# Second tile begun behind the first, a third unit ahead of the first tile, and weight steps placed behind the last bias

## The chip, the cores and the metric

One core of one Trainium2 chip runs the kernel. The metric is device microseconds of one launch. The engines are named as in the profile: PE is TensorE (matmul), PEld its weight load, DVE is VectorE, ACT is ScalarE, POOL is GpSimd, SP is the queue that issues most DMAs.

## What is computed

```python
# attention with random features, 4 batches, 8 heads, 576 rows, head size 64
def phi(x):
    proj = np.einsum('bhsd,md->bhsm', x, omega)
    sq = np.sum(x * x, axis=-1, keepdims=True) / 2.0
    h = proj - sq
    h = h - np.max(h, axis=-1, keepdims=True)
    return np.exp(h) / np.sqrt(m)
q_p, k_p = (phi(q_s), phi(k_s))
kv = np.einsum('bhsm,bhsd->bhmd', k_p, v)
z = np.sum(k_p, axis=2)
num = np.einsum('bhsm,bhmd->bhsd', q_p, kv)
den = np.einsum('bhsm,bhm->bhs', q_p, z)[..., None] + 1e-06
x = (num / den)                       # as 2304 rows of 512
# first network: 512 -> 2048 -> 512
h = x @ w_in
g = h * (1.0 / (1.0 + np.exp(-1.702 * h)))
x = g @ w_out
# second network: 512 -> 1536 -> 512
out = (x @ w_a) * (x @ w_b) @ w_out2
```

## The kernel before

Every product is made with numbers split in two halves of 16 bits, high and low: three matmuls (high by high, high by low, low by high) add up in one PSUM bank.

The rows of attention's result are cut in tiles: tile j (0 to 3) holds the first 512 rows of batch j, tile 4 the 256 rows that are left of all batches. The first network takes a tile in 16 units (`ffn1`, line 613). `h_products` (617) makes a unit's 12 matmuls, three for each of four chunks of xT, into a bank of the ring (two banks); chunk c of xT comes from part c (`hp`) of the Q phase. `h_unit` (627) adds the activation: tanh on ACT, `th` on DVE, `gh` on ACT, `gl` (the remainder) on DVE. `y_unit` (647) adds the unit to the tile's four sums y, 12 matmuls in the four banks of `ps_acc`. `main` (658) is a generator: y_unit(f), yield, h_unit(f + 2), yield. So two units are ahead. At the last two units there is no h_unit(f + 2); `main` then calls `after()`, which builds the next tile, and takes the next tile's first two units there. For the step from tile 0 to tile 1 (`j == 1`) these are split: chunks 0 to 2 of unit 0 behind y_unit(14), and its last chunk and unit 1 behind y_unit(15).

Attention of batch b + 1 runs beside tile b. `run` (1023) walks the tile's generator; after each yield it takes weight steps (`w_steps`) and one `side_step`, which moves each live phase of attention on by one yield. There are four K phases (`kphase32`) and four Q phases (`qphase`) in a batch, started two yields apart. Each begins with `features` (366): the input is split, transposed, squared and projected; `mx` is the row maximum (DVE, 470), `mh` and `nb` give the bias of the exponentials (DVE, 476), and ACT makes the exponentials (437). The projections go into one of the two banks of `ps_att` and the exponentials free it. The Q phase ends with the normalised result, whose transpose by DMA (603) writes xT. Batch 0's phases have run before tile 0; batch 1 is computed with the Q side in 32 bits, and its transposes of the exponentials are on PE.

Weights come as 34 chunks of 1 MB: 16 for `w_in` and `w_out` in turn (`NW1`), 4 for the first third of `w_a` and `w_b` (up to `NWE` = 20), 2 of the second network's output weights and 4 more of `w_a`, `w_b` (up to `NW2` = 26), and 8 later. The generator `w_ops` (203) converts them: `shift` (DVE, 214) and two passes that put the number's bits together (DVE, 254 and 262, on 128x1024), for the second network `sums` (DVE, 248), the high half on ACT (272), and the low half (DVE, 221). It yields four or five times for a chunk. `w_load` (196) issues the load on SP (line 200) into one of two buffers, two chunks ahead. `w_steps(n, upto)` takes n steps, `w_need(n)` all that are left up to chunk n. Tile 0 runs with one step at a yield, and so do tile 1 (to chunk 18, 12 steps) and tile 2 (to chunk 20, 10 steps), so that theirs are taken in the first yields, and tile 3 (to 26, 31 steps).

The framework that issues the program orders each engine's instructions itself, from the program's order and the dependencies. `tc.issue_after(ins)` adds that those instructions of the block that run on the engine of `ins` (here DVE) are queued behind `ins`; it adds no semaphore. In `run` it is used for tiles 1 and 2, with the last instruction of the batch before (`own["last", b - 1]`).

The second network (`ffn2`, 763) runs behind tile 4. A product's bank is copied by ACT into `ka`, `kb` (`keep`, 789), totals are added on DVE, and `ab_forms` (823) makes from two groups' results seven slots of high (ACT, 836) and low halves (DVE, 837), by `split` in pieces of two, two, two and one slot.

Of the kernel before, what the change touches and what calls it, by code (L numbers as in the profile page):

```python
# [9 lines left out]
F32 = mybir.dt.float32  # L10
# [23 lines left out]
def fused_kernel(  # L34
# [13 lines left out]
    nc = tc.nc  # L48
# [4 lines left out]
    P = 128  # L53
    NT = 4
    SM = NT * P
    SR = S - SM
    NHP = H // 2
    KC = DM // P
    FC1 = F1 // P
# [15 lines left out]
    first = ExitStack()  # L75
# [32 lines left out]
    RW = CW // P  # L108
# [58 lines left out]
    NW1 = len(chunks)  # L167
# [117 lines left out]
    def w_steps(n, upto):  # L285
        for _ in range(n):
            if w_done[0] < upto:
                w_done[0] = next(w_gen)

    def w_need(n):  # L290
        while w_done[0] < n:
            w_done[0] = next(w_gen)
# [73 lines left out]
    def features(pool, nm, x, e16, e32, psp, extra):  # L366
# [88 lines left out]
        for gi in range(len(GROUPS) + 2):  # L455
            if e32 is None:
                for gj in [x for x in es if x not in done]:
                    parts(gj)
                    done.append(gj)
            if 1 <= gi <= len(GROUPS):  # L460
                g, pv = GROUPS[gi - 1], pvs[gi - 1]
                pair = PAIRS[gi - 1]
                a, z = GROUPS[pair[0]][0], GROUPS[pair[-1]][-1] + 1
                if pair[0] not in mxs:
                    mxs[pair[0]] = [
                        pool.tile([P, T], F32, tag=t, name=f"{t}_{nm}_{gi}", bufs=2)
                        for t in ("mx", "mh", "nb")
                    ]
                mx, mh, nb = mxs[pair[0]]
                nc.vector.tensor_reduce(  # L470
                    out=mx[:, g[0] - a : g[-1] + 1 - a], in_=pv[:, : len(g), :], axis=AX.X, op=ALU.max
                )
                if gi - 1 == pair[-1]:

                    for o, i0, scale in ((mh, mx, PROJ), (nb, mh, -1.0)):
                        nc.vector.scalar_tensor_tensor(
                            out=o[:, : z - a], in0=i0[:, : z - a], scalar=scale, in1=sq[:, a:z],
                            op0=ALU.mult, op1=ALU.subtract,
                        )
                    for gj in pair:  # L480
                        exps(gj, nb, a)
            if gi < len(GROUPS):
                pvs[gi] = pv = psp().rearrange("p (t m) -> p t m", m=M)
                project(pv, GROUPS[gi])
            yield
# [127 lines left out]
    def ffn1(j, xh, xl, n):  # L613

        gh, gl, yacc, phs = {}, {}, {}, {}

        def h_products(f, cs):
            if f not in phs:
                phs[f] = ps_ring.tile([P, 512], F32, tag="ring", name=f"ph{j}_{f}")
            ph = phs[f]  # L620
            w, fs = w_in[f // 8], slice(f % 8 * P, (f % 8 + 1) * P)
            for c in cs:
                nc.tensor.matmul(ph[:, :n], w[:, 0, c, fs], xh(c), start=(c == 0), stop=False)  # L623
                nc.tensor.matmul(ph[:, :n], w[:, 0, c, fs], xl(c), start=False, stop=False)  # L624
                nc.tensor.matmul(ph[:, :n], w[:, 1, c, fs], xh(c), start=False, stop=(c == KC - 1))  # L625

        def h_unit(f, cs=range(KC)):
            h_products(f, cs)
            ph = phs.pop(f)
            th = mp.tile([P, 512], F32, tag="f32", name=f"th{j}_{f}")  # L630
            nc.scalar.activation(  # L631
                out=th[:, :n], in_=ph[:, :n], func=AF.Tanh, scale=0.5 * 1.702 / (S_X * S_W)
            )
            nc.vector.scalar_tensor_tensor(  # L634
                out=th[:, :n], in0=th[:, :n], scalar=1.0, in1=ph[:, :n], op0=ALU.add, op1=ALU.mult
            )
            GS = 0.5 * S_G / (S_X * S_W)
            a = gp.tile([P, 512], F16, tag="gh", name=f"gh{j}_{f}")
            b = gp.tile([P, 512], F16, tag="gl", name=f"gl{j}_{f}")
            nc.scalar.activation(out=a[:, :n], in_=th[:, :n], func=AF.Copy, scale=GS)  # L640
            nc.vector.scalar_tensor_tensor(  # L641
                out=b[:, :n], in0=th[:, :n], scalar=GS, in1=a[:, :n],
                op0=ALU.mult, op1=ALU.subtract,
            )
            gh[f], gl[f] = a, b

        def y_unit(f):
            w = w_out[f // 4]
            for c in range(KC):
                if f == 0:  # L650
                    yacc[c] = ps_acc.tile([P, 512], F32, tag="acc", name=f"y{j}_{c}")
                cs = slice(c * P, (c + 1) * P)
                o = yacc[c][:, :n]
                nc.tensor.matmul(o, w[:, 0, f % 4, cs], gh[f][:, :n], start=(f == 0), stop=False)  # L654
                nc.tensor.matmul(o, w[:, 0, f % 4, cs], gl[f][:, :n], start=False, stop=False)  # L655
                nc.tensor.matmul(o, w[:, 1, f % 4, cs], gh[f][:, :n], start=False, stop=(f == FC1 - 1))  # L656

        def main(after=None):

            following = None  # L660
            for f in range(FC1):
                w_need(2 * (f // RW) + 2)
                y_unit(f)
                if f + 1 == FC1:
                    yd = ydram.tile([P, KC, 512], F32, tag=f"y{j}", name=f"yd{j}")
                    for c in range(KC):
                        ye = mp.tile([P, 512], F32, tag="f32", name=f"ye{j}_{c}")
                        nc.scalar.activation(out=ye[:, :n], in_=yacc[c][:, :n], func=AF.Copy, scale=YS)
                        nc.sync.dma_start(out=yd[:, c, :n], in_=ye[:, :n])
                    ys[j] = yd  # L670
                yield
                if f + 2 < FC1:
                    w_need(2 * ((f + 2) // RW) + 1)
                    h_unit(f + 2)
                    yield
                elif after is not None:
                    if following is None:
                        following = after()
                    _, last_rows, products, unit = following
                    if not last_rows:  # L680
                        unit(f + 2 - FC1)
                    elif f + 2 == FC1:
                        products(0, range(KC - 1))
                    else:
                        unit(0, (KC - 1,))
                        unit(1)
                    yield

        return main, j == 1, h_products, h_unit

# [70 lines left out]
    def ffn2():  # L763
# [59 lines left out]
        def ab_forms(k):  # L823
# [9 lines left out]
                nc.vector.tensor_tensor(out=o[:, :n], in0=x[:, :n], in1=y[:, :n], op=op)  # L833

            def split(slots, x):
                nc.scalar.copy(t[:, 0, slots], x)  # L836
                nc.vector.tensor_tensor(out=t[:, 1, slots], in0=x, in1=t[:, 0, slots], op=ALU.subtract)

            put(cb[:, 0], ca[:, 1], ca[:, 2], ALU.add)
# [180 lines left out]
    def begin(t, gen):  # L1020
        waiting.append((turn[0] + t, gen))

    def run(gen, wn=0, wmax=0, after=None):
        for _ in gen:
            if after is None:
                w_steps(wn, wmax)
            else:
                with tc.issue_after(after):
                    w_steps(wn, wmax)
            side_step()  # L1030

    def finish_side():
# [29 lines left out]
    def xparts(xT):  # L1062
        return lambda c: xT[:, c, 0, :], lambda c: xT[:, c, 1, :]
# [27 lines left out]

    following = []

    def next_tile(make):
        def made():
            finish_side()
            following.append(make())
            return following[-1]

        return made  # L1100

    xT = x_tile(0, zp, "z")
    with tc.tile_pool(name="att", bufs=2) as att:
# [18 lines left out]
        fillers(FILL)  # L1122
        w_steps(POST_W, NW1)
        following.append(ffn1(0, *xparts(xT), SM))
        _, _, products, unit = following[0]
        w_need(1)
        for f in range(2):
            products(f, range(KC - 1))
        for f in range(2):
            unit(f, (KC - 1,))  # L1130
        for b in range(1, B):
            x1 = x_tile(b, zp, "z")
            begin_k(b, att, psp_att, 0, AL, b == 1)
            begin_q(b, att, x1, psp_att, NHP * AL, AL, b == 1)
            last = own["last", b - 1]
            run(
                following[-1][0](next_tile(lambda: ffn1(b, *xparts(x1), SM))),
                1, (NW1, NW1 + 2, NWE)[b - 1], last.ins if b > 1 else None,
            )
    late["pool"] = ctx.enter_context(tc.tile_pool(name="late", bufs=1))  # L1140
    run(following[-1][0](next_tile(rest_tile)), 1, NW2)
    w_need(NW2)
    y_load(0, SM)
    fg = y_forms(0, SM)
    for _ in following[-1][0]():
        next(fg, None)
    for _ in fg:
        pass
    first.close()
    late["sums"] = ctx.enter_context(tc.tile_pool(name="sums", bufs=1, side="right", reuse_waits="tile"))  # L1150
    ffn2()
# [36 lines left out]
```

## Time and profile before

| | |
|---|---|
| median of 3 runs | 920.68 us (918.95 to 921.78) |
| profiled execution | 919.44 us |
| its span | 917.7 us |
| granted PE clock, mean | 0.998 |
| busy: PE, DVE, ACT | 885.5, 679.0, 442.0 us |

The profiled execution's time is the span and 1.74 us around it. Busy times of PE overlap from one matmul to the next; idle times don't. A wait is written as "engine tile line <- who released it: us in total, times, longest". Attention of batch 0 fills the first 58 us; tile 0 goes to about 190 us, tile 1 to 298, tile 2 to 406, tile 4 ends at 532, and the second network takes the rest.

### The profile page before, as it was taken

Reading aid. Unit: us, or ns where it says so; the run is one execution under the profiler, and the core shown is the slowest. Engines: PE = TensorE matmul, PEld = TensorE weight load, DVE = VectorE, ACT = ScalarE, POOL = GpSimd, SP = SyncE. Lnnn points to the kernel's source line nnn. Section 1 sums busy time; section 2 is a strip of 40 time slices with the busy share of each in tenths; the row PEclk is TensorE's granted clock in tenths of the full one; section 3 lists DMA queues with packets and bytes.
Section 4 is the critical chain, followed back from the end, with each engine's and each line's share of the span. In section 5 each row is a group of like instructions: output and inputs, shape, how many; then the busy total and the mean of one; then the engine's idle time right before and its main releaser. Section 6 shows DMA issues by size and latency. Waiting matters only on the chain.

```text
span 917.7 us, 17145 instructions
## 1 busy us (share of the span) xinstructions
PE 885.5 (96%) x6984; PEld 639.0 (70%) x6984; DVE 679.0 (74%) x1220; ACT 442.0 (48%) x1047; POOL 1.7 (0%) x11
## 2 busy tenths in 40 slices
PE   8989999989999999999999999999999999999997
PEld 6864555635654466544447888888988888988886
DVE  5889998488678966779932389876999567566756
ACT  6675787556664566554423355543543232233221
POOL 0000000000000000000000000000000000000000
PEclk9999999999999999999999999999999999999999
DMA  7855578263576524554421043223330122223312
GB/s 180 230 146 170 169 224 265 74 104 72 133 151 136 177 56 72 95 141 136 182 82 46 1 162 119 103 90 121 128 126 11 72 41 82 81 93 127 75 47 70
DMA packets 129344, 105.35 MB, mean 115 GB/s; under 512 B 97777, under 2 KB 111089, under 8 KB 127217
## 3 DMA queue, kind: packets, MB, share of 16 engines
q1 hardware_dynamic: 128960, 103.96, 40.2%
q8 instruction: 55, 0.90, 0.4%
q10 hardware_dynamic: 304, 0.30, 0.1%
q14 instruction: 25, 0.20, 0.1%
HBM read 71.07 MB, written 17.69 MB: 97 GB/s over the span
## 4 chain that ended last, share of the span: by engine, by line
PE 54%; DVE 28%; ACT 7%; DMA 6%; issue 4%; SPq 0%; ACTq 0%; DVEq 0%
PE y L654 3%; PE y L655 3%; PE ph L623 3%; PE ph L624 3%; PE y L656 3%; PE ph L625 3%; PE pa L503 2%; DVE wf L254 2%; DVE wf L262 2%; DMA xt_k<-x_k 2%; DVE ca L810 2%; DVE sx L248 2%; PE oA L880 2%; PE oA L878 2%; DVE th L634 2%
## 5 line engine op out<-in xcount | busy, mean ns | idle before, releaser
L655 PE MATMUL y<-gl,w_out 128*128 128x512 f16 (+1 forms) x320 | 114.3, 358 | 2.0 <-DVE gl L641 2.0
L656 PE MATMUL y<-gh,w_out 128*128 128x512 f16 (+1 forms) x320 | 114.3, 358 | 0.0
L654 PE MATMUL y<-gh,w_out 128*128 128x512 f16 (+1 forms) x320 | 111.7, 358 | 0.1
L623 PE MATMUL ph<-xT,w_in 128*128 128x512 f16 x256 | 97.5, 381 | 3.0 <-DMA xT<-x_q_2x 1.4
L624 PE MATMUL ph<-xT,w_in 128*128 128x512 f16 x256 | 97.5, 381 | 0.3 <-DVE xT L592 0.3
L625 PE MATMUL ph<-xT,w_in 128*128 128x512 f16 x256 | 97.5, 381 | 0.0
L634 DVE SCALAR_TENSOR_TENSOR th<-th,ph 128x512 f32<-128x512 f32 (+1 forms) x80 | 50.2, 629 | 53.9 <-ACT th L631 53.9
L631 ACT ACTIVATE th<-ph 128x512 f32<-128x512 f32 (+1 forms) x80 | 44.5, 557 | 68.1 <-PE ph L625 67.9
L640 ACT ACTIVATE gh<-th 128x512 f16<-128x512 f32 (+1 forms) x80 | 46.8, 586 | 48.4 <-DVE th L634 48.1
L785 PE MATMUL paA<-forms,w_a 128*128 128x256 f16 (+1 forms) x240 | 60.9, 262 | 2.6 <-ACT ka L793 2.3
L886 DVE SCALAR_TENSOR_TENSOR o<-oA,o 128x512 f32<-128x512 f32 (+1 forms) x45 | 28.5, 634 | 46.3 <-PE oA L880 46.2
L785 PE MATMUL pbA<-forms,w_b 128*128 128x256 f16 (+1 forms) x240 | 61.1, 262 | 1.1 <-DVE cb L804 1.0
L641 DVE SCALAR_TENSOR_TENSOR gl<-th,gh 128x512 f16<-128x512 f32 (+1 forms) x80 | 50.5, 633 | 15.0 <-ACT gh L640 14.9
L787 PE MATMUL pbA<-forms,w_b 128*128 128x256 f16 (+1 forms) x240 | 61.0, 262 | 0.0
L786 PE MATMUL pbA<-forms,w_b 128*128 128x256 f16 (+1 forms) x240 | 61.0, 262 | 0.0
L787 PE MATMUL paA<-forms,w_a 128*128 128x256 f16 (+1 forms) x240 | 61.0, 262 | 0.0
L786 PE MATMUL paA<-forms,w_a 128*128 128x256 f16 (+1 forms) x240 | 61.0, 262 | 0.0
L878 PE MATMUL oA<-w_o,ab 128*128 128x256 f16 x216 | 58.9, 273 | 1.7 <-ACT ab L836 0.9
L880 PE MATMUL oA<-w_o,ab 128*128 128x256 f16 x216 | 58.9, 273 | 0.2
L879 PE MATMUL oA<-w_o,ab 128*128 128x256 f16 x216 | 58.9, 273 | 0.0
L624 PEld LDWEIGHTS <-w_in 128*128 128x128 f16 x320 | 31.6, 99 | 31.1 <-issue 4.5
L656 PEld LDWEIGHTS <-w_out 128*128 128x128 f16 x320 | 31.3, 98 | 31.0 <-issue 3.9
(195 smaller groups left out, 2302.4 us busy)
## 6 DMA issues: line engine op xcount, KB each, us to landing
wraw<-in_moe_w_out_dram SPq DMA_DIRECT2D x14, 1024.0 KB
forms<-fd SPq DMA_DIRECT2D x8, 1792.0 KB
wraw<-in_moe_w_in_dram SPq DMA_DIRECT2D x8, 1024.0 KB
fd<-forms SPq DMA_DIRECT2D x4, 1792.0 KB
wraw<-in_moe_w_a_dram SPq DMA_DIRECT2D x6, 1024.0 KB
wraw<-in_moe_w_b_dram SPq DMA_DIRECT2D x6, 1024.0 KB
rawk<-in_k_dram SPq DMA_DIRECT2D x16, 256.0 KB
vt<-in_v_dram SPq DMA_DIRECT2D x16, 256.0 KB
```

The source lines that it names most:

```text
L623: nc.tensor.matmul(ph[:, :n], w[:, 0, c, fs], xh(c), start=(c == 0), stop=False)
L624: nc.tensor.matmul(ph[:, :n], w[:, 0, c, fs], xl(c), start=False, stop=False)
L625: nc.tensor.matmul(ph[:, :n], w[:, 1, c, fs], xh(c), start=False, stop=(c == KC - 1))
L634: nc.vector.scalar_tensor_tensor(out=th[:, :n], in0=th[:, :n], scalar=1.0, in1=ph[:, :n], op0=ALU.add, op1=ALU.mult)
L654: nc.tensor.matmul(o, w[:, 0, f % 4, cs], gh[f][:, :n], start=(f == 0), stop=False)
L655: nc.tensor.matmul(o, w[:, 0, f % 4, cs], gl[f][:, :n], start=False, stop=False)
L656: nc.tensor.matmul(o, w[:, 1, f % 4, cs], gh[f][:, :n], start=False, stop=(f == FC1 - 1))
L785: nc.tensor.matmul(o[:, i], wh, xh, start=first, stop=False, skip_group_check=True)
L786: nc.tensor.matmul(o[:, i], wh, xl, start=False, stop=False, skip_group_check=True)
L787: nc.tensor.matmul(o[:, i], wl, xh, start=False, stop=final, skip_group_check=True)
L878: nc.tensor.matmul(bank[:, t], lh, wh, start=first, stop=False, skip_group_check=True)
L880: nc.tensor.matmul(bank[:, t], ll, wh, start=False, stop=final, skip_group_check=True)
```

## The change

1. The `nb` instruction is kept in `own["nb"]`, and `run` queues the DVE instructions of every weight step behind the last `nb` made so far, for all tiles (before: tiles 1 and 2 alone, behind the last instruction of the batch before).
2. `run` takes a rate in place of a count: 1 step a yield in tile 0, 11/32 in tiles 1 and 2, 22/32 in tile 3; tile 4 takes a step at every second yield, and `w_need(NW2)` moves from before tile 4 to behind it.
3. `head` makes a tile's first units: the products of all of them without the last chunk, then the last chunks. Tile 0 gets three units in it; the third has a bank of `ps_acc`, and `w_need` for its weights goes before it. `main(first=3)` then leaves h_unit(2) out.
4. Tile 0 runs to its end without `after`; tile 1 is built and its two units made behind it, with `head`.
5. `split` in `ab_forms` copies each slot by an ACT instruction of its own.

```diff
@@ features
-                        nc.vector.scalar_tensor_tensor(
+                        own["nb"] = nc.vector.scalar_tensor_tensor(
                             out=o[:, : z - a], in0=i0[:, : z - a], scalar=scale, in1=sq[:, a:z],
                             op0=ALU.mult, op1=ALU.subtract,
-                        )
+                        ).ins
@@ ffn1
-        def h_products(f, cs):
+        def h_products(f, cs, pool=ps_ring, tag="ring"):
             if f not in phs:
-                phs[f] = ps_ring.tile([P, 512], F32, tag="ring", name=f"ph{j}_{f}")
+                phs[f] = pool.tile([P, 512], F32, tag=tag, name=f"ph{j}_{f}")
...
-        def main(after=None):
+        def main(after=None, first=2):
...
-                if f + 2 < FC1:
+                if first <= f + 2 < FC1:
                     w_need(2 * ((f + 2) // RW) + 1)
                     h_unit(f + 2)
                     yield
-                elif after is not None:
+                elif f + 2 >= FC1 and after is not None:
                     if following is None:
                         following = after()
-                    _, last_rows, products, unit = following
-                    if not last_rows:
-                        unit(f + 2 - FC1)
-                    elif f + 2 == FC1:
-                        products(0, range(KC - 1))
-                    else:
-                        unit(0, (KC - 1,))
-                        unit(1)
+                    following[2](f + 2 - FC1)
                     yield
@@ ab_forms
             def split(slots, x):
-                nc.scalar.copy(t[:, 0, slots], x)
+                for i in range(slots.stop - slots.start):
+                    nc.scalar.copy(t[:, 0, slots.start + i], x[:, i])
@@ run
-    def run(gen, wn=0, wmax=0, after=None):
+    def run(gen, rate, wmax):
+        due = 0.0
         for _ in gen:
-            if after is None:
-                w_steps(wn, wmax)
-            else:
-                with tc.issue_after(after):
-                    w_steps(wn, wmax)
+            due += rate
+            with tc.issue_after(own["nb"]):
+                w_steps(int(due), wmax)
+            due -= int(due)
             side_step()
@@ new
+    def head(tile, units):
+        _, products, unit = tile
+        for f in range(units):
+            w_need(2 * (f // RW) + 1)
+            if f < 2:
+                products(f, range(KC - 1))
+            else:
+                products(f, range(KC - 1), ps_acc, "acc")
+        for f in range(units):
+            unit(f, (KC - 1,))
@@ the tiles
-        _, _, products, unit = following[0]
-        w_need(1)
-        for f in range(2):
-            products(f, range(KC - 1))
-        for f in range(2):
-            unit(f, (KC - 1,))
+        head(following[0], 3)
         for b in range(1, B):
...
-            last = own["last", b - 1]
-            run(
-                following[-1][0](next_tile(lambda: ffn1(b, *xparts(x1), SM))),
-                1, (NW1, NW1 + 2, NWE)[b - 1], last.ins if b > 1 else None,
-            )
+            ahead = next_tile(lambda: ffn1(b, *xparts(x1), SM))
+            if b == 1:
+                run(following[-1][0](first=3), 1, NW1)
+                ahead()
+                head(following[-1], 2)
+            else:
+                run(following[-1][0](ahead), 11 / 32, (NW1 + 2, NWE)[b - 2])
     late["pool"] = ctx.enter_context(tc.tile_pool(name="late", bufs=1))
-    run(following[-1][0](next_tile(rest_tile)), 1, NW2)
-    w_need(NW2)
+    run(following[-1][0](next_tile(rest_tile)), 22 / 32, NW2)
     y_load(0, SM)
     fg = y_forms(0, SM)
-    for _ in following[-1][0]():
+    for i, _ in enumerate(following[-1][0]()):
         next(fg, None)
+        if i % 2:
+            w_steps(1, NW2)
     for _ in fg:
         pass
+    w_need(NW2)
```

## Rows read from the trace of the kernel before

**Rows 1.** The page's first part: TensorE's busy us, share, instructions.

```profile
PE 885.5 (96%) x6984; PEld 639.0 (70%) x6984; DVE 679.0 (74%) x1220; ACT 442.0 (48%) x1047; POOL 1.7 (0%) x11
```

**Rows 2.** Busy us by stretch: stretch, length, each engine, granted clock, DMA share, GB/s.

```profile
92.00:119.00 27.00, 24.81 (x162) 14.41 (x162) 24.62 (x40) 20.65 (x83) 0.00 (x0) 1.00 0.61 182
119.00:170.00 51.00, 50.59 (x332) 29.21 (x330) 42.89 (x79) 34.84 (x126) 0.00 (x0) 1.00 0.71 204
...
192.00:222.00 30.00, 27.36 (x151) 13.17 (x151) 25.90 (x50) 17.23 (x37) 0.00 (x0) 1.00 0.48 98
222.00:290.00 68.00, 66.71 (x527) 38.95 (x526) 46.26 (x119) 40.37 (x108) 0.00 (x0) 1.00 0.59 117
...
400.00:460.00 60.00, 58.58 (x270) 26.20 (x268) 58.93 (x91) 29.95 (x51) 0.00 (x0) 1.00 0.53 174
460.00:531.00 71.00, 70.93 (x517) 50.32 (x515) 21.15 (x43) 21.61 (x47) 0.00 (x0) 1.00 0.10 35
```

**Rows 3.** TensorE's waits, 58 to 70 us: total, times, longest.

```profile
PE pa L590 <- DVE xf_q L562: 1.1, 1, 1.1
PE ph L623 <- DVE th L634: 0.6, 1, 0.6
```

**Rows 4.** TensorE's waits, 60 to 190 us, on the exponentials.

```profile
PE pa L406 <- ACT e_k L437: 2.3, 3, 0.9
```

**Rows 5.** TensorE's waits, 170 to 192 us, on DMAs.

```profile
PE ph L623 <- DMA xT<-x_q_2x: 1.4, 1, 1.4
PE ph L623 <- DMA xT<-x_q_3x: 0.9, 1, 0.9
...
PE pa L406 <- DMA xt_k<-x_k: 0.5, 1, 0.5
```

**Rows 6.** TensorE's longest waits, 190 to 480 us.

```profile
PE pa L406 <- ACT e_k L437: 3.4, 3, 1.9
PE y L655 <- DVE gl L641: 2.0, 4, 0.6
```

**Rows 7.** TensorE's wait on the copies ka, in the second network.

```profile
PE paA L785 <- ACT ka L793: 2.3, 6, 0.6
```

**Rows 8.** VectorE in order of time at the first tile's start: start, us.

```profile
65.30 1.21 DVE L221 SCALAR_TENSOR_TENSOR w_in<-wf,w_in 128x1024 f16<-128x1024 f32 x1
...
67.57 1.27 DVE L634 SCALAR_TENSOR_TENSOR th<-th,ph 128x512 f32<-128x512 f32 x2
```

**Rows 9.** VectorE in order of time, a bias of batch 1.

```profile
88.41 0.15 DVE L476 SCALAR_TENSOR_TENSOR mh_k<-mx_k,sq_k 128x5 f32<-128x5 f32 x1
88.49 1.21 DVE L262 SCALAR_TENSOR_TENSOR wf<-wraw,wf 128x1024 int32<-128x1024 int32 x1
89.62 0.15 DVE L476 SCALAR_TENSOR_TENSOR nb_k<-mh_k,sq_k 128x5 f32<-128x5 f32 x1
```

**Rows 10.** All engines at the change to tile 1, columns as in rows 2.

```profile
186.20:188.90 2.70, 2.61 (x6) 0.86 (x6) 2.64 (x5) 1.23 (x3) 0.00 (x0) 0.50 0.35 68
```

**Rows 11.** VectorE in order of time, a weight pass in batch 2's K phase.

```profile
210.72 1.22 DVE L254 SCALAR_TENSOR_TENSOR wf<-wraw,wf 128x1024 int32<-128x1024 int32 x1
```

**Rows 12.** Line 262 alone by stretch: length, VectorE busy, passes.

```profile
92.00:119.00 27.00, 4.88 (x4) 1.00 0.61 182
119.00:170.00 51.00, 6.08 (x5) 1.00 0.71 204
```

**Rows 13.** ScalarE's copies by shape: busy us, mean ns, idle before.

```profile
L836 ACT CAST ab<-ca 128x1024 f16<-128x1024 f32 x24 | 24.4, 1044 | 12.7 <-DVE ca L833 10.6 <-DVE ca L810 1.9
...
L836 ACT CAST ab<-cb 128x512 f16<-128x512 f32 x15 | 9.3, 619 | 17.6 <-DVE cb L833 17.6
```

**Rows 14.** SP in order of time, the last transpose of batch 2.

```profile
289.45 1.23 SPq L603 DMA_TRANSPOSE xT<-x_q_3x  x1
```

**Rows 15.** The chain that ended last, in order of time, at 186 us.

```profile
186.83 3.09 DMA xT<-x_q_3x
```

**Rows 16.** TensorE in order of time, first use of that transpose.

```profile
296.07 0.38 PE L623 MATMUL ph<-xT,w_in 128*128 128x512 f16 x1
```

More of the change, by code (lines that the diff above doesn't have):

```diff
@@ L675, in main @@
                     yield
-                elif after is not None:
+                elif f + 2 >= FC1 and after is not None:
                     if following is None:
                         following = after()
-                    _, last_rows, products, unit = following
-                    if not last_rows:
-                        unit(f + 2 - FC1)
-                    elif f + 2 == FC1:
-                        products(0, range(KC - 1))
-                    else:
-                        unit(0, (KC - 1,))
-                        unit(1)
+                    following[2](f + 2 - FC1)
                     yield
-        return main, j == 1, h_products, h_unit
+        return main, h_products, h_unit
     tiles = [(j, SM) for j in range(B)] + [(B, 2 * P)]
```

## The prediction

> **What bounds the kernel now.** The page's first part comes first: TensorE is busy 885.5 of 917.7 us, VectorE 679.0, ScalarE 442.0 [rows 1]. So TensorE is the bound in the mean, and what a change can give back is what TensorE idles; a matmul's busy time is longer than the distance to the next one, so the idle time alone is read. Then the stretches one by one [rows 2]. In tile 0, at the start of tile 1 and through tile 3 the engine that is full is VectorE: 24.62 of 27 us at 92 to 119, 25.90 of 30 at 192 to 222, 58.93 of 60 at 400 to 460. In between it has room: 46.26 of 68 us at 222 to 290, and 21.15 of 71 at 460 to 531. The reader is to see that the conversion of the weights (three integer passes, sums and a remainder on VectorE) is bunched where attention's K phase runs, and absent where VectorE is two thirds busy.
>
> Then the waits of TensorE, stretch by stretch, which are the list of all that can be won: 1.1 and 0.6 us at the first tile's start [rows 3], 2.3 us on the exponentials of K in batch 1 [rows 4], 1.4, 0.9 and 0.5 us at the change from tile 0 to tile 1 [rows 5], 3.4 us on the exponentials of K in batches 2 and 3 and 2.0 us on gl, the remainder of the activations, in tiles 1 to 3 [rows 6], 2.3 us on the copy ka in the second network [rows 7]. None is long; together they are 14.5 us, with the slow clock below some 16 of 919.
>
> **The change part by part.** The sum is made against the profiled execution, 919.44 us (917.7 span and 1.74 around it). It lies 1.24 us under the median of 920.68, and that is added at the end.
>
> *Third unit ahead.* 12 matmuls of unit 2 (9 of them before the last chunk of xT) move in front of y_unit(0); nothing is added. They can fill the 1.1 us before the transposes of the last q part and replace the 0.6 us that unit 2 now waits for th to free its ring bank [rows 3]. The first needs the low half of the second w_in chunk, which VectorE makes at 65.30 [rows 8], behind the hole. To come earlier it has to pass the last xT remainder, and then delays that by its own 1.21 us. The unit's bank is one of y's four, so y_unit(0)'s fourth column now waits for unit 2's th, with the whole TensorE queue behind it; that wait is of the kind that is now 0.6 us. Taken: 0.6 us won, between 1.3 lost and 1.7 won.
>
> *Weights behind the last bias, batch 1.* A dependent VectorE pair (mh, then nb) has a pause between its two instructions, and a conversion pass stands in it: mh at 88.41, a pass of 1.21 us, nb at 89.62 [rows 9]. Such a pass stands in 8 of batch 1's 16 pairs, between 78 and 146 us, 8.7 us in all, and in two of batch 2's. The exponentials wait for nb and they free the two attention banks, and TensorE waits for those 2.3 us [rows 4]. The new edge puts the passes behind the last nb that is already issued. It cannot help where a pass was issued before the nb, and about half the passes are forced by w_need, outside it. Taken: half, 1.2 us; between 0 and 2.3.
>
> *Second tile behind the first.* unit 0's and 1's products of tile 1 are issued after y_unit(15) instead of around it. In the trace TensorE had run y_unit(15) well before, and waited for xT's chunks 2 and 3 with all the other products done; at 186.2 to 188.9 its granted clock is 0.50 (the 1.2 GHz level), and the six matmuls there fill 2.61 us, which at the full clock would be 1.3 [rows 10]. The hole is 1.4+0.9+0.5 us [rows 5], with the clock 4.1 us. The order alone doesn't close it; only an attention chain of batch 1 that ends earlier does, by the 8.7 us of passes that stand in it now. TensorE hides most of these, so I take a third: 1.3 us. At the other end, a pass of tile 1's weights may now start in this stretch (the old edge held them to the batch's last instruction) and delay the chain by 1.2 us. Between 1.2 lost and 4.1 won.
>
> *Weights spread and behind the bias, batches 2 and 3, tile 3.* Today the 12 and 10 steps are taken in the first yields of the tile; a pass of 1.22 us at 210.72 stands ahead of the K maximum and the bias [rows 11], and TensorE waits 3.4 us for the exponentials (1.9 the longest) and 2.0 us for gl [rows 6]: 5.4 us. At 11 steps in 32 yields a third of the passes is left in that stretch. Taken: 3.5 us; between 0 and 5.4. Their loads go with them: the SP instruction of a load isn't tied by the edge, but waits for the pass that frees its buffer, and the transposes and the K and Q loads queue behind it. Tile 0 has such waits now, and the one hole that a transpose of K leaves is 0.5 us [rows 5]; it is inside the bounds. GpSimd has no part.
>
> *What the moved steps cost where they go.* At most four chunks come to stand in the Q phases of batches 2 and 3. Batch 1 shows what a chunk costs beside attention: 27-24.81 us idle with four second passes at 92 to 119, which is 0.55 us each; 51-50.59 us with five at 119 to 170, 0.08 each [rows 2, 12]. So 0.3 to 2.2 us; I take 1.0, nearer the second, since VectorE's load there is nearer to it. The nine steps that go to tile 4 cost nothing under the cover of VectorE's 50 idle us at 460 to 531; without it they would be nine passes of 1.2 us, 11 us.
>
> *ScalarE's split copies.* 45 more instructions. They let the copy ka, which frees a bank, in sooner: 2.3 us are waited for it now [rows 7], and with a blocking copy of half the length half of it goes, 1.15 us. A copy of 1024 columns takes 1.044 us, of 512 0.619 [rows 13]: 0.19 us for each extra one, 8.6 us of an engine that is half idle. On the path they stand only in the last group, three of them, 0.57 us. Net 0.6 won, between 0.6 lost and 1.7 won. The Trainium skill (ScalarE: Activation LUTs, What ACT_TABLE_LOAD costs) gives an ACTIVATE with immediate operands 186 ns of fixed time, and 93 ns of overlap between neighbours; by that an extra copy costs 0.093 us, 4.2 us for the 45 and 0.28 us in the last group, and the sum would be 6.5 instead of 6.2. The rule speaks against the split, the durations speak twice as strongly.
>
> **Sum:** 0.6+1.2+1.3+3.5-1.0+0.6 = 6.2 us. 919.44-6.2 = 913.2; with 1.24 for the median 914.5.
>
> **The rivals.**
> *Nothing that can be measured, 920.7.* The holes move instead of closing. For it: each is under 2 us and has two engines in series behind it; where the bias comes sooner, ScalarE, busy 20.65 of 27 us at 92 to 119 [rows 2], still has its own queue ahead of the exponentials. Against it: VectorE is the engine with the higher share in just the stretches with holes.
> *Slower, 926.8.* The passes that now stand in the Q phases hold up the chain of batch 2 and 3 until the change of tiles stalls, as it does today from tile 0 to 1. The transpose of batch 2's last chunk is issued at 289.45 [rows 14], such a one lands 3.09 us later [rows 15], at 292.5, and is first needed at 296.07 [rows 16]: 3.5 us of slack. Some 7 of the 11 steps fall in the Q phase. It decides from 0.5 us of delay a step: at a whole pass, 1.2 us each, the chain is 8.4 us late, the hole 4.9 and the clock another 1.3, and for batch 3, taken alike, the same: 12.4 us more, 913.2+12.4+1.2 = 926.8. Against it: at 119 to 170 passes stand among batch 1's Q phases and TensorE idles 0.41 us [rows 2].
> *Much faster, 909.8.* Tile change and K phases close entirely: 2.8 and 1.9 us more than taken. For it: VectorE idles 21 us at 222 to 290 [rows 2], more than what moves there.
> *The change doesn't do what it says:* unit 2 can't start before its weights are ready at 66.5, and nothing is ahead. That is the 0.6 us of the first term and stays in the forecast.
>
> **How the numbers follow.** Forecast 0.52, nothing 0.24, slower 0.16, much faster 0.08. Half widths of the terms (1.5, 1.2, 2.7, 2.8, 1.0, 1.2) are independent; the root of their squares' sum is 4.6, so 910 to 919 for the likeliest case alone. To hold 8 in 10 the range reaches up past the case of nothing, 920.7 with the 1 us that the runs of before scatter, and down to the much faster one: 908.5 to 921.5. About 0.3%, 2.8 us, is what a measurement of this kernel tells from no change: faster 0.60, same 0.24, slower 0.16.
>
> **What would show it.** Right: no conversion pass between mh and nb in batches 2 and 3, few in batch 1; TensorE's waits on e_k in batches 2 and 3 gone; VectorE under 8 tenths of 192 to 222 and over 7 of 222 to 290; waits on ka halved; conversion passes after 460. Wrong: a wait of TensorE on xT's last chunk at the change to tile 2 or 3, with the clock at half; new waits on gl in 222 to 290; unit 0's th later than the 67.57 us at which it starts now [rows 8]; or a hole at 186 that has only grown, which would mean that the order of the second tile's beginning itself counts and not the chain before it.

## The result

The changed kernel takes 929.44 us (929.18 to 931.61) beside 920.58 us: ratio 1.0103 [1.0081, 1.0125]. It is slower by some 9 us where 6 us were forecast to be won, and the time lies outside the range.

Where the time went is read first from the starts of the y products (line 654) in TensorE's order of time. The table has profiled executions; such a start scatters by about 2 us between executions: in e9 below, whose tile 0 is that of the kernel before to the instruction, tile 1 begins at 195.4 and not at 193.3.

| start, us | before | after |
|---|---|---|
| tile 0, first unit | 69.4 | 70.5 |
| tile 0, unit 8 | 119.5 | 129.2 |
| tile 0, last unit | 170.3 | 195.0 |
| tile 1, first unit | 193.3 | 204.1 |
| tile 2, 3, 4, first unit | 301.9, 409.8, 492.1 | 310.8, 418.2, 501.3 |
| span | 917.7 | 927.3 |

All of it, 10.8 us, is lost before tile 1; tile 1 gives 1.9 back (106.7 us instead of 108.6, no more than such a time scatters, as e6 shows below), and everything behind is as long as it was, within 1 us. So the result is a story of tile 0 alone. The stretches of after, columns as in [rows 2]:

```profile
92.00:119.00 27.00, 21.00 (x142) 12.27 (x140) 19.49 (x35) 19.20 (x86) 0.00 (x0) 1.00 0.42 121
119.00:170.00 51.00, 42.77 (x267) 25.27 (x266) 35.57 (x65) 31.16 (x117) 0.00 (x0) 0.90 0.75 186
170.00:205.00 35.00, 34.20 (x200) 19.62 (x201) 27.41 (x53) 19.82 (x38) 0.00 (x0) 1.00 0.58 150
192.00:222.00 30.00, 29.24 (x149) 13.66 (x148) 16.42 (x31) 16.03 (x30) 0.00 (x0) 1.00 0.35 78
222.00:290.00 68.00, 66.07 (x511) 38.83 (x510) 51.78 (x125) 43.67 (x119) 0.00 (x0) 1.00 0.61 138
400.00:460.00 60.00, 58.07 (x280) 26.23 (x279) 58.44 (x99) 30.57 (x52) 0.00 (x0) 1.00 0.63 199
460.00:531.00 71.00, 71.00 (x476) 46.39 (x475) 29.43 (x51) 21.61 (x45) 0.00 (x0) 1.00 0.15 51
```

From 92 to 170 TensorE idles 14.2 us, before 2.6 [rows 2], and VectorE, which was to be the full engine there, idles with it: 22.9 us, before 10.5. Two engines that idle together may be waiting for each other; e12 below tests it. TensorE's granted clock is 0.90 at 119 to 170, before 1.00: by that mean some 10 of the 51 us are at the lower of its two levels (1.2 and 2.4 GHz). By the two rates that e12 and e13 show below, where the same matmuls take 5.5 and 3.1 us, an estimate of what this cost, as part of the loss, is at most 4 to 5 us. TensorE's waits of after, 60 to 205 us (total, times, longest):

```profile
PE pa L406 <- ACT e_q L437: 4.7, 3, 2.0
PE pa L406 <- ACT e_k L437: 4.0, 4, 1.4
PE pa L526 <- DVE xf_q L562: 2.2, 1, 2.2
...
PE ph L623 <- ACT w_in L272: 1.1, 2, 0.7
...
PE ph L625 <- DVE w_in L221: 0.7, 2, 0.4
```

The waits on the exponentials, which the edge was to shorten, have grown: on e_k from 2.3 us [rows 4] to 4.0, and on e_q from 0.4 to 4.7. The converted weights themselves (w_in, 1.8 us) are waited for too. The hole at the change of tiles [rows 5] isn't there any more, since so much of tile 0 is left that TensorE has work. Three engines of after in order of time, one pass through the loop: VectorE, then ScalarE, then TensorE (start, us, idle before):

```profile
95.89 0.16 DVE L476 SCALAR_TENSOR_TENSOR nb_k<-mh_k,sq_k 128x4 f32<-128x4 f32 x1
95.97 2.35 DVE L262 SCALAR_TENSOR_TENSOR wf<-wraw,wf 128x1024 int32<-128x1024 int32 x2
98.24 0.28 DVE L470 TENSOR_REDUCE mx_k<-pa 128x1 f32<-128x128 f32 x1
98.44 1.21 DVE L221 SCALAR_TENSOR_TENSOR w_in<-wf,w_in 128x1024 f16<-128x1024 f32 x1
```

```profile
96.15 1.14 ACT L437 ACTIVATE e_k<-pa,nb_k 128x128 f32<-128x128 f32 x4 [0.97 <-DVE nb_k L476]
97.22 1.06 ACT L272 ACTIVATE w_in<-wf 128x1024 f16<-128x1024 f32 x1
```

```profile
97.34 0.22 PE L406 MATMUL pa<-om_h,xt_k 128*128 128x128 f16 x1 [0.92 <-ACT e_k L437]
...
98.34 0.39 PE L623 MATMUL ph<-xT,w_in 128*128 128x512 f16 x1 [0.72 <-ACT w_in L272]
...
99.72 0.39 PE L625 MATMUL ph<-xT,w_in 128*128 128x512 f16 x1 [0.34 <-DVE w_in L221]
```

Two conversion passes start the moment the nb is through; ScalarE makes w_in's high half 1.3 us later, VectorE the low half, and TensorE waits for the exponentials, for the high and for the low half in turn. In the kernel before line 262's passes for w_in and w_out, sixteen in all, are some 4 to 10 us apart from 66 us on; here they come in pairs behind an nb (95.97, 116.84, 138.1, 161.9), and the last two only at 176.8 and 184.9, where before the last was at 149.8.

### The profile page after: what moved, and what is told of

Its sections match the earlier page's. It is cut to its first block, busy times and chain, and to the rows that moved or that the text cites. A ratio compares the mean times of both kernels' runs of the same rounds, so it can differ in the third digit from the quotient of the medians.

```text
span 927.3 us, 17190 instructions
## 1 busy us (share of the span) xinstructions
PE 888.1 (96%) x6984; PEld 641.5 (69%) x6984; DVE 677.6 (73%) x1220; ACT 446.2 (48%) x1092; POOL 1.7 (0%) x11
## 4 chain that ended last, share of the span: by engine, by line
PE 63%; DVE 22%; ACT 7%; DMA 5%; issue 3%; SPq 0%; ACTq 0%; DVEq 0%
PE ph L623 4%; PE ph L624 4%; PE ph L625 4%; PE y L655 4%; PE y L654 4%; PE y L656 4%; PE pa L503 2%; PE pa L533 2%; PE oA L872 2%; PE oA L874 2%; PE oA L873 2%; DVE wf L254 2%; PE paA L778 2%; PE pbA L780 2%; PE pbA L778 2%
## 5 line engine op out<-in xcount | busy, mean ns | idle before, releaser
L830 ACT CAST ab<-ca 128x512 f16<-128x512 f32 (+1 forms) x60 | 32.7, 574 | 43.8 <-DVE ca L803 29.1
```

## The experiments

The theory after the first look: *the edge in tile 0 carries the loss*, because passes that tile 0 itself needs are queued behind a bias that waits for TensorE. The rivals: the third unit (its bank is one of y's), the order of the second tile, and the edge's bunching of passes. Each kernel was timed beside the kernel before; its median is 921.7, 921.0, 921.3, 921.2 and 921.3 in the five groups. Microseconds of a gain or loss are the ratio's, taken of 921.

**e1, after, tile 0's steps free of the edge; e2, before, with the edge on tile 0 alone; e3, after with two units ahead; e4, before with tiles 1 to 4 spread.**

```diff
 e1: run(gen, rate, wmax, free=False)
+            if free:
+                w_steps(int(due), wmax)
+            else:
...
 e2: run(...)
-                with tc.issue_after(after):
+                with tc.issue_after(own["nb"] if after == "nb" else after):
...
-                1, (NW1, NW1 + 2, NWE)[b - 1], last.ins if b > 1 else None,
+                1, (NW1, NW1 + 2, NWE)[b - 1], last.ins if b > 1 else "nb",
 e3: two units
-        head(following[0], 3)
+        head(following[0], 2)
...
-                run(following[-1][0](first=3), 1, NW1)
+                run(following[-1][0](), 1, NW1)
 e4: the kernel before with after's run (tile 0 free at rate 1)
+                1 if b == 1 else 11 / 32, (NW1, NW1 + 2, NWE)[b - 1], free=b == 1,
...
+    run(following[-1][0](next_tile(rest_tile)), 22 / 32, NW2)
...
+        if i % 2:
+            w_steps(1, NW2)
```

> The changed kernel, but tile 0's weight steps are not queued behind the last bias; everything else of the change stays. Edge theory (the edge in tile 0 holds the conversion passes of weights that tile 0 itself needs, so TensorE runs out of converted weights and tile 1's first y matmul comes at 204.1 us instead of 193.3): 918 to 920 us, first y of tile 1 at 192 to 195, TensorE's waits on w_in and on the exponentials at 60 to 180 us fall from 9.8 to about 3 us. Third-unit theory (unit 2 in a bank of y and its earlier weights upset tile 0): 928 to 931. Theory that the later tiles' spreading or the split copies cost the time: 928 to 931.

> The kernel before with one thing added: tile 0's weight steps are queued behind the last bias. Edge theory: 928 to 933 us, passes of line 262 in tile 0 in pairs right behind a bias, y units of tile 0 at uneven distances of up to 20 us. All other theories: 919 to 922, as before.

> The changed kernel without the third unit: two units ahead of tile 0 as before, all else changed. Edge theory: 928 to 932. Third-unit theory: 919 to 923.

> The kernel before with the changed weight steps of tiles 1 to 4 alone (spread at 11/32 and 22/32, behind the last bias, nine steps in tile 4); tile 0, its head, the change to tile 1 and the copies as before. My prediction's term for this was 3.5 won less 1.0: 918. Edge theory: 917.5 to 920.5, since between the first y of tile 1 and the last y the changed kernel took 335.8 us and the kernel before 337.3. Theory that the later tiles' spreading costs the time: 926 or more.

e1 took 918.63 us, 0.9971 [0.9955, 0.9987] of the kernel before: without the edge on tile 0 the change is a small gain, 2.7 us, and the edge costs about 11 (929.4-918.6 is 10.8, by the ratios it is 12.2). Its tile 1 begins at 195.2. The two kernels' lines 262 and 221 (the last pass of a chunk) between 84 and 172.5 and from there to 195, after first, then e1, columns as in [rows 12]. For each stretch line 262's row comes first and then line 221's; in e1 neither line has a pass behind 172.5, so the last row stands for both:

```profile
84.00:172.50 88.50, 9.49 (x8) 0.94 0.63 162
84.00:172.50 88.50, 10.19 (x9) 0.94 0.63 162
172.50:195.00 22.50, 2.40 (x2) 1.00 0.40 119
172.50:195.00 22.50, 2.41 (x2) 1.00 0.40 119
```

```profile
84.00:172.50 88.50, 12.16 (x10) 1.00 0.66 189
84.00:172.50 88.50, 13.38 (x11) 1.00 0.66 189
172.50:195.00 22.50, 0.00 (x0) 0.92 0.55 121
```

Two chunks of sixteen are late by the end of attention's biases. e2 took 925.32, 1.0038 [1.0025, 1.0051]: the edge alone makes the kernel before slower, by 3.5 us. At the start of tile 1 it costs 8.0 us there (201.3 to 193.3) and 8.9 in after (204.1 to 195.2), nearly the same; but in e2 tile 1 then takes 106.1 us instead of 108.6, while e1 and after are alike there (107.1 and 106.7). By the spans the edge costs 5.4 us in e2 (923.1-917.7) and 9.8 in after (927.3-917.5), and these two places are 3.0 of the 4.4 between them. The times are further apart, 3.5 and about 11. The granted clock at 119 to 170 is 0.97 in e2 and 0.90 in after, which by the same estimate is at most some 3 us more in after; no run separates it, and why the edge costs more in after is left open. e3 took 928.17, 1.0062 [1.0037, 1.0086]: without the third unit most of the loss stays, so the third unit isn't the cause. Whether it makes the edge dearer can't be told, as that interval just meets the changed kernel's [1.0081, 1.0125]. e4 took 920.01, 0.9994 [0.9979, 1.0009]: the term that was to carry the gain gives nothing that can be told. Its tile 1 takes 107.0 us instead of 108.6 and its tile 3 83.1 instead of 82.3. The first can't be put down to the spread: with the steps of tile 1 as before, tile 1 takes 106.8 in e6 and 109.1 in e9.

**e5, the second tile behind the first alone; e6, the third unit alone; e7, after, tile 0's steps behind the nb of two yields earlier; e8, after with all of tile 0's steps held** (at two a yield few are left to be forced by w_need).

```diff
 e5: before
+            ahead = next_tile(lambda: ffn1(b, *xparts(x1), SM))
...
+            if b == 1:
+                ahead()
+                _, _, products, unit = following[-1]
+                for f in range(2):
+                    products(f, range(KC - 1))
+                for f in range(2):
+                    unit(f, (KC - 1,))
 e6: before with h_products(f, cs, pool, tag), main(after, first) and
+        for f in range(3):
+            w_need(2 * (f // RW) + 1)
...
 e7: run(gen, rate, wmax, lag=0), lag=2 in tile 0
+            seen.append(own["nb"])
-            with tc.issue_after(own["nb"]):
+            with tc.issue_after(seen[max(0, len(seen) - 1 - lag)]):
 e8:
-                run(following[-1][0](first=3), 1, NW1)
+                run(following[-1][0](first=3), 2, NW1)
```

> The kernel before with one thing added: tile 0 runs to its end and tile 1's two units are made behind it. Theory that the order alone does nothing (the hole at the change is the attention chain's end): 919.5 to 922.5, first y of tile 1 within 1 us of 193.3, TensorE's waits on xT's chunks 2 and 3 still 2 to 4 us. Theory that the order closes the hole: 915 to 918 with no wait on xT. If it costs beside the edge what the changed kernel lost more than the edge alone: 923 or more.

> The kernel before with one thing added: three units ahead of tile 0, the third in a bank of y. My prediction's term: 0.6 us won, 920.5. Third-unit theory: 922 to 925, first y matmul later than 69.4 by about 1 us because three activations stand in front of it, and that delay kept at the first y of tile 1.

> The changed kernel, but tile 0's steps are queued behind the bias that was the last one two yields earlier. Edge theory (the time lost is the time for which passes wait for a bias): between the two, 920 to 926, first y of tile 1 between 195 and 203. If only the presence of an edge counts, not how late its bias is: 928 to 931.

> The changed kernel with two steps a yield in tile 0, so that all its steps are taken ahead of their need and all of them stand behind a bias, in place of about half. If the loss comes from steps held behind a bias: 930 to 940. If it comes from steps being taken too late in the program, which two a yield would cure: 918 to 924.

e5: 921.61, 1.0009 [0.9994, 1.0023]. e6: 919.69, 0.9983 [0.9968, 0.9998]. e7: 923.88, 1.0030 [1.0017, 1.0044]. e8: 932.12, 1.0119 [1.0092, 1.0145]. So the order makes no difference that can be told, the third unit wins 1.6 us, and the loss follows how tightly the passes are held: 918.6 free, 923.9 behind an older nb, 929.4 behind the last, 932.1 with every step held (the last two aren't told apart by their intervals). In e8 the passes of line 262 are evenly spaced (89.8, 100.2, 112.3, 122.6) and the loss is no smaller, so the bunching isn't what costs. There TensorE waits for the low halves themselves:

```profile
PE pa L406 <- ACT e_k L437: 4.1, 5, 1.3
PE pa L406 <- ACT e_q L437: 4.0, 4, 1.3
PE ph L625 <- DVE w_in L221: 3.6, 2, 2.8
```

**e9, the split copies alone; e10, before with the third unit and the spread in tiles 1 and 2; e11, e7 with the nb of six yields earlier.**

```diff
 e9: before
-                nc.scalar.copy(t[:, 0, slots], x)
+                for i in range(slots.stop - slots.start):
+                    nc.scalar.copy(t[:, 0, slots.start + i], x[:, i])
 e10: e6 with run(gen, wn, wmax, held)
+                1 if b == 1 else 11 / 32, (NW1, NW1 + 2, NWE)[b - 1], b > 1,
 e11:
+                run(following[-1][0](first=3), 1, NW1, lag=6)
```

> The kernel before with one edit: the second network's copies are cut slot by slot. The prediction's term says 0.6 us won (0.6 lost to 1.7 won): about 920.4 beside 921 for the kernel before. The second network's length in the profiles so far (387.1 before, 387.4 after, 387.1 without the split in e4, 386.7 with it in e1) says nothing won or lost: 921, within 0.5.

> The kernel before with two edits: tile 0 begins with three units and leaves its steps free, and the steps of tiles 1 and 2 are taken at 11 in 32 yields behind the last nb; order of the second tile, tiles 3 and 4, and the copies are as before. If the pieces add up as the milestones say (third unit 1.3 won as in e6, 1 to 2 won in tiles 1 and 2 as in e4, whose tile 3 gave 0.8 back), about 918.5 beside 921. If the third unit and the spread win the same time, 919.7, as with the third unit alone.

> The changed kernel, but tile 0's steps are queued behind the nb of six yields earlier instead of the last one. If the loss is what a conversion pass waits behind a bias that isn't there yet, a bias that old has nearly always been made, and the time goes on down from 929.4 (last nb) and 923.9 (two yields earlier) to 918.5 to 920.5, the time without the edge. If the loss comes from the edge's fixing of VectorE's order as such, whichever bias it names, it stays at 923 to 925.

e11: 918.99, 0.9980 [0.9965, 0.9995]. An edge to a bias that is long made costs nothing; so what costs is the wait, not that the order is fixed. e10: 918.51, 0.9969 [0.9955, 0.9983]; with e1 it is the fastest kernel here, and faster than both the kernel before and the changed one. e9: 920.48, 0.9994 [0.9980, 1.0008], which doesn't tell a gain of 0.6 us from none; its second network takes 386.7 us in the profile, before 387.1. The wait on ka hasn't halved but grown; first e9, then after:

```profile
PE paA L785 <- ACT ka L793: 3.7, 6, 1.1
```

```profile
PE paA L778 <- ACT ka L786: 4.1, 6, 1.4
```

The wait on the split copies themselves (ab, 0.9 us before) is gone, and that on ca has grown from 0.2 to 1.4 us; in sum the second network's waits of 0.2 us and more are 5.1 us before and 6.2 in e9.

**e12, after, with tile 0's weights ready.** To open the loop at one point, tile 0's units take weights again and again that are converted early: w_in's of unit f modulo 2 (the expectation below says four), w_out's of f modulo 4. All chunks are loaded and converted as in after; tile 0's results are those of other weights. (One line more: h_products is at 624 to 626, th at 635, gl at 642.)

```diff
-            w, fs = w_in[f // 8], slice(f % 8 * P, (f % 8 + 1) * P)
+            u = f % RW if j == 0 else f
+            w, fs = w_in[u // 8], slice(u % 8 * P, (u % 8 + 1) * P)
...
-            w = w_out[f // 4]
+            w = w_out[0 if j == 0 else f // 4]
```

> The changed kernel, edge and all, but tile 0's units take the first four units' weights again and again (unit f those of f modulo 4), which are ready before tile 0 begins; every chunk is still loaded and converted in its place behind the last nb. Tile 0's results are those of other weights. If the loss is a loop (passes wait for the bias, the bias waits for TensorE, TensorE waits for weights that are not converted), the loop is open: tile 0 no longer falls behind, its last unit begins before 178 us instead of at 195, and the time is 916 to 921. If the edge costs by what it does to VectorE's own queue (the activation's th and gl, the attention's steps), with weights or without, tile 0 stays late and the time is 926 to 931.

It took 925.09, 1.0036 [1.0024, 1.0048], which neither reading gave. Half of the first came true: TensorE is busy 49.42 us at 119 to 170, and tile 0's last unit begins at 170.2, not at 195.0. So late weights are why tile 0 falls behind. But tile 1 still begins at 203.4, and waits for attention (this profiled execution, 927.31 us, is the longest of its nine and 2.2 us above their median, so its times may be late by about that):

```profile
92.00:119.00 27.00, 26.34 (x177) 15.42 (x176) 21.07 (x37) 20.95 (x95) 0.00 (x0) 1.00 0.44 126
119.00:170.00 51.00, 49.42 (x316) 28.28 (x313) 39.49 (x72) 33.95 (x122) 0.00 (x0) 1.00 0.77 194
170.00:205.00 35.00, 26.73 (x139) 17.13 (x139) 24.07 (x49) 16.82 (x33) 0.00 (x0) 0.76 0.57 143
```

```profile
PE ph L624 <- DMA xT<-x_q_3x: 4.1, 1, 4.1
```

VectorE there, in order of time, shows a second way: passes left over from the tile stand between the steps (dd, rc, xf) that make the last Q parts' results, each of which something waits for.

```profile
172.59 0.17 DVE L476 SCALAR_TENSOR_TENSOR nb_q<-mh_q,sq_q 128x5 f32<-128x5 f32 x1
172.67 1.30 DVE L214 TENSOR_SCALAR wf<-wraw 128x1024 int32<-128x1024 int32 x2
173.88 1.23 DVE L254 SCALAR_TENSOR_TENSOR wf<-wraw,wf 128x1024 int32<-128x1024 int32 x1
175.61 0.17 DVE L557 TENSOR_SCALAR dd_q<-pa 128x5 f32<-128x5 f32 x1 [0.50 <-PE pa L533]
175.69 1.22 DVE L262 SCALAR_TENSOR_TENSOR wf<-wraw,wf 128x1024 int32<-128x1024 int32 x1
176.82 0.18 DVE L561 RECIPROCAL rc_q<-dd_q 128x5 f32<-128x5 f32 x1
176.92 1.18 DVE L254 SCALAR_TENSOR_TENSOR wf<-wraw,wf 128x1024 int32<-128x1024 int32 x1
178.02 0.48 DVE L562 TENSOR_TENSOR xf_q<-pa,rc_q 128x320 f32<-128x320 f32 x1
178.42 1.21 DVE L221 SCALAR_TENSOR_TENSOR w_in<-wf,w_in 128x1024 f16<-128x1024 f32 x1
```

**e13, e12 with tile 0's steps free (`free` as in e1); e14, e12 with the edge, but the last two chunks converted in tile 1.**

```diff
 e13:
+                run(following[-1][0](first=3), 1, NW1, free=True)
 e14: main
+                w_need(min(2 * (f // RW) + 2, NW1 - 2 if j == 0 else NW1))
...
-                run(following[-1][0](first=3), 1, NW1)
+                run(following[-1][0](first=3), 1, NW1 - 2)
...
+                run(following[-1][0](ahead), (20 if b == 2 else 11) / 32, (NW1 + 2, NWE)[b - 2])
```

> The run before (tile 0's units take the first units' weights, ready from the start) with tile 0's steps free of the edge. Tile 0's results are those of other weights. It is the footing for that run: if the edge's cost is passes that come late, and these then stand among the last Q part's own steps on VectorE, freeing them brings tile 1's start from 203 back to 195 and the time to 916 to 919.5. If weights that are ready cost something of their own (TensorE taken from attention earlier), tile 1 still starts after 200 and the time stays at 922 to 926.

> The same with the edge kept, but tile 0 stops converting two chunks short of its 16; these two are converted in tile 1 (20 instead of 11 steps in its 32 yields), which is the first to use them. Tile 0's results are those of other weights. If the rest of the edge's cost is the some 10 us of passes that were left over behind the last nb and stand between the last Q part's steps, tile 1 starts at 194 to 198 instead of 203.4 and the time is 916 to 920.5. If it is the held passes before the last nb that make the Q part late, tile 1 starts after 200 as before and the time is 923 to 927.

e13: 922.02, 1.0002 [0.9982, 1.0023]; e14: 925.36, 1.0039 [1.0027, 1.0051]. Both missed. e13 shows that ready weights cost some 3 us of their own against e1 (922.0 and 918.6): tile 0 ends earlier (166.9 to 170.2), attention's last nb comes at 174.1 instead of 171.7, its tail then has TensorE to itself and runs at a lower granted clock, and tile 1 begins at 199.2. On that footing the edge costs 3.1 us (925.1-922.0, give or take 2 by the intervals) where tile 0 doesn't have to wait for its weights, against about 11 where it does. So some 8 of the 11 us go through the late weights of tile 0, and some 3 another way. This split holds for these four kernels: with weights ready it is attention's tail that tile 1 waits for, with late ones tile 0's own work. e14 has 4.9 us of conversion passes between 172.5 and 195 where e12 has 10.4: tile 1 begins at 200.5 instead of 203.4, 2.9 of the 4.2 us that separate e12 from e13. In the time it gives nothing, since its tile 2 takes 110.1 us where e12's and e13's take 106.8 and 106.7; this wasn't followed further.

The left-over passes are not all of those 4.2 us. The last transpose to xT (line 603) is issued at 194.6 in e12, 191.8 in e14 and 192.8 in e13, so the last Q part is 1.8 us later in e12 than in e13. The other 2.4 us come behind it: the same 23 matmuls from that transpose's landing to tile 1's first y product run at the lower clock level in e12 (and in e14) and at the upper one in e13. e12 first, then e13, columns as in [rows 2]:

```profile
196.60:203.40 6.80, 5.51 (x23) 2.72 (x23) 3.93 (x7) 4.12 (x8) 0.00 (x0) 0.50 0.72 144
192.70:199.20 6.50, 3.12 (x23) 1.60 (x23) 4.24 (x8) 3.98 (x8) 0.00 (x0) 1.00 0.68 143
```

That the left-over passes delay the last Q part is thus seen in traces (e12 beside e13 and e14), by not much more than such starts scatter, and not in a time.

## Why the prediction was wrong

**The step that failed** is the term "Weights behind the last bias, batch 1", with its "Taken: half, 1.2 us; between 0 and 2.3". It priced what the passes did to the bias, and not what the bias does to the passes. It counted the forced half of the passes as lying outside the edge; but a chunk's last pass works on what the first has made, so a held first pass holds the forced ones too: line 262's eight passes between 92 and 170 all stand in pairs behind an nb. Tile 0 converts its own weights just in time, and each pass has TensorE behind it. A lower bound of 0 had no reason beside it: who waits for line 262's passes (w_in's high half on ScalarE, then line 623 on TensorE) would have shown that a loss was possible. What the runs showed in place of 1.2 us won: VectorE idles 12.4 us more than before at 92 to 170 and TensorE 11.6, and the term measured about 11 us lost in after, 3.5 in the kernel before. What it was to do it did in part: a pass stands between mh and nb in 5 of batch 1's 16 pairs in after, in 8 before.

**The first reading** was off as well. It names VectorE as the full engine of three stretches; in the same rows [rows 2] TensorE is busy 24.81, 27.36 and 58.58 us there, beside VectorE's 24.62, 25.90 and 58.93. So VectorE was not the fuller of the two in the first two, and to move its work was not sure to give time back.

**The rival "slower, 926.8"** came out near the time by luck, since its way is another. It placed the stall in the Q phases of batches 2 and 3, and no wait on xT at the change to tile 2 or 3 is in the trace. In tiles 1 to 3 the steps make weights for the second network, long before their need, and there the edge costs nothing that can be told (e4).

**Third unit:** 0.6 won was taken, between 1.3 lost and 1.7 won; e6 measured 1.6 won, with an interval from 0.2 to 2.9. In after, unit 0's th did come later, at 69.03 us instead of 67.57 [rows 8], a sign that was listed as wrong; it is repaid by unit 1, whose y products begin at 73.5 in both.

**Second tile behind the first:** 1.3 won was taken; e5 measured 0.8 lost, between 2.1 lost and 0.6 won. "The order alone doesn't close it" was right; the earlier attention that was to close it didn't come: batch 1's last nb is at 173.3 us in after and 171.7 in e1, 171.0 before, and in e1 TensorE's waits on xT at the change are 2.8 and 1.0 us, before 0.9 and 1.4 [rows 5].

**Spread, batches 2 and 3, tile 3:** 3.5 won less 1.0 was taken; e4 measured about 0.6, not to be told from nothing. The signs that were listed are there: VectorE falls from 25.90 to 16.42 of 30 us at 192 to 222 and rises to 51.78 of 68 at 222 to 290, no pass stands between mh and nb in batches 2 and 3, and passes run behind 460. The waits didn't follow. In after, 190 to 480 us:

```profile
PE pa L406 <- ACT e_k L437: 2.0, 2, 1.0
PE y L655 <- DVE gl L641: 1.9, 3, 1.0
```

1.5 us of the 5.4 of [rows 6] went. The order of work was right and the size was not: the passes stood beside those waits, and most of the waits stayed when the passes had gone. This is the rival "nothing", right for this part.

**Split copies:** 0.6 won was taken; e9 measured 0.6 won, between 1.8 won and 0.7 lost, so neither the term nor nothing is ruled out. Its working failed, though. The price of the extra copies was nearly double, and the halved wait on ka didn't come. Two copies of 512 columns in a row take 1.14 us in e9, one of 1024 took 1.044 [rows 13]:

```profile
583.54 1.14 ACT L837 CAST ab<-ca 128x512 f16<-128x512 f32 x2
```

So an extra copy costs 0.10 us, not the 0.19 that the single durations gave. Two single copies of 0.619 us would be 1.24 in sum, and take 0.10 less in a row. Here the Trainium skill (ScalarE: Activation LUTs, What ACT_TABLE_LOAD costs) was the better source: it has neighbours overlap by about 93 ns, and the trace agrees with 0.10 us. Which of the two prices holds can't be seen in the time.

**The sum:** alone, the third unit, the order, the spread and the split came to 2.0 us won (1.6-0.8+0.6+0.6), and e1, which has all four, to 2.7. The parts without the edge on tile 0 add up within their scatter; the forecast of 6.2 was too high by what the spread and the order didn't bring, and then the edge took some 11. Each of these is known to 1 or 2 us only.

## What to carry to other kernels

Before a step is queued behind another, ask of the step itself when it is due and who waits for it: an order edge is free where the step has slack or the other is long done, as six yields back, and can close a loop where the step feeds the engine that the other waits for. A bound of zero loss for an edge needs a reason of its own. And a wait that stands beside an engine's full stretch is won only if the trace shows that the work to be moved ends that wait.

## What the runs showed of the hardware

That TensorE's dense work ended early was no gain here, where only a thin chain was left behind it: in e13 tile 0's last unit begins 3.3 us sooner than in e1 and tile 1 4.0 us later, with the granted clock at 0.80 in 170 to 195 against 0.93. The two rows, e13 first, columns as above:

```profile
170.00:195.00 25.00, 19.08 (x112) 14.05 (x110) 12.33 (x32) 9.89 (x25) 0.00 (x0) 0.80 0.31 71
```

```profile
170.00:195.00 25.00, 19.93 (x128) 12.60 (x127) 14.08 (x35) 13.29 (x29) 0.00 (x0) 0.93 0.50 109
```

The means lie between the levels of 1.2 and 2.4 GHz; in e13 TensorE had made 112 matmuls in these 25 us, in e1 128. Not all of the 4.0 us can be the clock: attention's last nb, at 174.1 in e13 and 171.7 in e1, is 2.4 us late already. How much the clock adds behind it no run separates. Where the same work stands at either level, in e12 and e13 above, 23 matmuls took 5.51 us at 0.50 and 3.12 at 1.00.
